# Cutting a key block's column products and summing product in two pieces each in a fused attention and Mish kernel

## The chip, the cores and the metric

The kernel runs on one core of a Trainium2 chip. The metric is the device time of one execution in microseconds (us), taken as the median of several runs.

## The reference

The input x is [1, 2048, 512]. One block normalises it and feeds two branches, which are multiplied and added back to x:

```python
xn = layernorm(x)                                   # over the 512 columns, no gain
q = (xn @ wq).reshape(1, 2048, 32, 16)              # 32 heads of 16
k, v = xn @ wk, xn @ wv                             # one key and one value head, 16 wide
p = softmax(einsum("bhqd,bkd->bhqk", q, k) * 16 ** -0.5)
s = (p @ v, heads side by side) @ wo
g = silu(mish(xn @ w1 + b1) @ w2)                   # 512 -> 1792 -> 512
out = x + s * g
```

All tensors are float32.

## The kernel before, in words

The work falls into a lead-in, 512 steps, and a short tail. A step (`s` in the code) takes one key tile of 128 keys for one unit; there are 32 units, each four heads by 512 queries. Per step TensorE computes four score products (tile `e`, line 1098), ScalarE turns them into exponentials (`pt`, line 1100), and TensorE multiplies the `pt` of two steps before with the values (`pv`, line 1187). The softmax needs row maxima ahead of the scores: TensorE computes score products a second time with the sides changed over (tile `m`, line 1119; the name `m_a_n` carries the half a and the count n) and VectorE takes the maximum of each (`mb`, line 1123), four per step, 20 steps ahead of their use.

Between these products TensorE works off groups of products for the other matrices (tile `xps`): query projections (weights `wq`), the first Mish matrix (weights `ws`, held in `early` for a while), the second (`wbs` with `act`), and the output matrix. A group has 12 or 15 products. In the lead-in each is one instruction over 128 rows (line 116). In the steps each is cut into two products over 64 rows (line 120), here called half-products, which share the array with an `m` or an `e` of the other 64 rows.

The lead-in loads x in four column blocks of 512 tokens (block 0 to 3), normalises (ScalarE, `xin`), transposes on TensorE (`xp`, line 302), copies the transposes into `xf` (line 320), and makes the keys and values of the block. For block 0 that is `k_proj`: four products into one bank. For blocks 1 to 3 it is

- `k_part` (line 336): 8 products with 32 output rows each, four column tiles of the array at a time, in two halves of 256 tokens, into the bank `kq`;
- `k_stage` (line 341): ScalarE copies `kq` to `vt`;
- `k_sum` (line 345): one product `ksum` x `vt` over 512 tokens into the bank `kp`, which adds up the four column tiles;
- `k_high` on ScalarE (line 356) and `k_low` on VectorE (line 239), which write the key block into `ks`; `v_copy`, `v_transpose` (`vp`) and `v_out` (`vaug`) for the values.

`kq`, `kp` and `vp` share one bank (`ps_v`). Maxima have three banks of their own (`ps_m`) and are taken in the order of the list `MSEQ`: eight of unit 0 on block 0, two of unit 1, then the rest of unit 0, eight to a key block, then unit 1. Each entry is a pair, one `m` for each half a. The lead-in ends when all 32 pairs of unit 0 are taken: VectorE makes the rows of maxima (`mp`, `cr`), eight DMAs carry them into `qt` (line 1174), and the first `e` can run.

What TensorE, ScalarE, VectorE, GpSimd and the DMA queue do in the lead-in, and in which order, is set by a planner at the end of the function. It holds tasks with an engine, an estimated duration and dependencies (`task(engine, us, function, deps, ...)`), keeps a clock `T` for each engine, and emits at each turn the task that can start first. A pair of maxima ("M") goes ahead of a task of TensorE when it may start no later; where TensorE has nothing for over 0.35 us by these estimates, the planner emits three products of the next group ("X") or, where no group is ready, a product whose result nobody reads (`warm`, line 1434). `bank(tag, n, t, users)` makes a task wait until the bank's earlier users are through. After the lead-in the order of the steps comes from other rules (`waves`), which take over the group where it stands.

```python
        if m is not None and (b is None or m <= b[0] + 0.05 or T["DVE"] < T["PE"] + 0.3 and m <= T["PE"] + 0.1):
            opts.append((m, "PE", "M"))
        elif b:
            opts.append((b[0], "PE", b[1]))
        e0 = min((o for o in opts if o[1] == "PE"), default=None, key=lambda o: o[0])
        low = min((o[0] for o in opts), default=None)
        if e0 is None or e0[0] > T["PE"] + 0.35:
            opts.append((T["PE"], "PE", "X"))
```

Of the kernel before, what the change touches and what calls it, by code (L numbers as in the profile page):

```python
# [14 lines left out]
F32 = mybir.dt.float32  # L15
# [5 lines left out]
P = 128  # L21
# [6 lines left out]
C = 512  # L28
# [98 lines left out]
def block_kernel(ctx: ExitStack, tc: tile.TileContext, x, wq, wk, wv, wo, w1, b1, w2, out):  # L127
# [5 lines left out]
    ps_v = ctx.enter_context(tc.tile_pool(name="ps_v", bufs=1, space=bass.MemoryType.PSUM))  # L133
# [4 lines left out]
    pe, act, dve, pool, sp = nc.tensor, nc.scalar, nc.vector, nc.gpsimd, nc.sync  # L138
# [27 lines left out]
    def sub(eng, o, a, b):  # L166
        ew(eng, o, a, b, ALU.subtract)
# [8 lines left out]
    def f(ap):  # L176
        return ap.bitcast(F32)
# [77 lines left out]
    def norm_a(z):  # L255
        if z.start >= 8:
            charge(0.25)
            pool.tensor_scalar(ve[:, z], mvs[:, z, 1], 1.0 / D if z.start >= A_LO else 1.0, EPS, op0=ALU.mult, op1=ALU.add)
        elif z.start >= A_LO:
            dve.tensor_scalar(ve[:, z], mvs[:, z, 1], 1.0 / D, EPS, op0=ALU.mult, op1=ALU.add)  # L260
        else:
            dve.tensor_scalar(ve[:, z], mvs[:, z, 1], EPS, None, op0=ALU.add)

    def norm_b(z):
        act.activation(rstd[:, z], ve[:, z], AF.Ln)
        act.activation(rstd[:, z], rstd[:, z], AF.Exp, scale=-0.5)

    def norm_c(z):
        r, h, b = rstd[:, z], hv[:, z], nbias[:, z]
        if z.start >= 8:  # L270
            charge(1.1)
            pool.tensor_tensor(out=h, in0=ve[:, z], in1=r, op=ALU.mult)
            pool.tensor_tensor(out=h, in0=h, in1=r, op=ALU.mult)
            pool.tensor_scalar(h, h, -0.5, 1.5, op0=ALU.mult, op1=ALU.add)
            pool.tensor_tensor(out=r, in0=h, in1=r, op=ALU.mult)
            if z.start < A_LO:
                pool.tensor_scalar(b, mvs[:, z, 0], -1.0, 0.0, op0=ALU.mult, op1=ALU.add)
            pool.tensor_tensor(out=b, in0=b, in1=r, op=ALU.mult)
            return
        stt(h, ve[:, z], -0.5, r, ALU.mult, ALU.mult)  # L280
        mul(dve, h, h, r)
        stt(r, h, 1.5, r, ALU.add, ALU.mult)
        if z.start >= A_LO:
            mul(dve, nbias[:, z], nbias[:, z], r)
        else:
            stt(nbias[:, z], mvs[:, z, 0], -1.0, r, ALU.mult, ALU.mult)

    def x_scale(t):
        x_ = xin[divmod(t, 4)]
        if t < 4 and t % 2:  # L290
            dve.tensor_scalar(x_, x_, rstd[:, t:t + 1], nbias[:, t:t + 1], op0=ALU.mult, op1=ALU.add)
        else:
            xn_scale(x_, x_, t)
# [3 lines left out]
    def x_transpose(t):  # L297
        c, tt = divmod(t, 4)
        ps, tag = (ps_m, "m") if t == 3 else (ps_e, "e")
        xp_of[t] = ps.tile([P, NDT, P], F32, tag=tag, name=f"xp{t}")  # L300
        for dt in range(NDT):
            pe.transpose(xp_of[t][:, dt], xin[c, tt][:, P * dt:P * (dt + 1)], ident)  # L302
# [7 lines left out]
    def x_high(t):  # L310
        act.activation(x_part(t, 0), xp_of[t], AF.Copy)
# [3 lines left out]
    def x_copy(t):  # L315
        c, tt = divmod(t, 4)
        if tt == 0:
            xf_of[c] = [sb.tile([P, 2, C], F32, tag="act", name=f"xf{c}_{k}", bufs=NACT) for k in range(2)]
        for k in range(2):
            act.activation(xf_of[c][k][:, :, P * tt:P * (tt + 1)], xp_of[t][:, 2 * k:2 * k + 2], AF.Copy)  # L320

    def x_low(t):
        sub(dve, x_part(t, 1), xp_of[t], f(x_part(t, 0)))

    vt_of = {}

    kp_of = {}
    kq_of = {}
    vp_of = {}

    def k_part(c):
        kq = ps_v.tile([P, C], F32, tag="v", name=f"kq{c}")
        for h in range(2):
            z = slice(C // 2 * h, C // 2 * (h + 1))
            for dt in range(NDT):
                pe.matmul(kq[32 * dt:32 * dt + 32, z], wkf[:, dt, P - 32:P], xf_of[c][dt // 2][:, dt % 2, z], start=True, stop=True)
        kq_of[c] = kq

    def k_stage(c):
        vt_of[c] = sb.tile([P, C], F32, tag=f"y{(2, 3, 1, 2)[c]}", name=f"vt{c}", bufs=1)  # L340
        act.activation(vt_of[c], kq_of[c], AF.Copy)

    def k_sum(c):
        kp_of[c] = ps_v.tile([P, C], F32, tag="v", name=f"kp{c}")
        pe.matmul(kp_of[c], ksum, vt_of[c], start=True, stop=True)

    def k_proj(c, dts):
        if 0 in dts:
# [30 lines left out]
    ksum = wkv[:, P:2 * P]  # L379
# [636 lines left out]
    def xt_keep(c):  # L1016

        xt_kept[c] = dram.tile([P, NDT, C], F32, tag=f"xt{c}", name=f"xtk{c}")
        for k in range(2):
            sp.dma_start(xt_kept[c][:, 2 * k:2 * k + 2], xf_of[c][k])  # L1020
# [284 lines left out]
    def task(eng, us, fn, deps=(), **kw):  # L1305
        t = Task(eng, us, fn, deps, **kw)
        plan[eng].append(t)
        return t
# [45 lines left out]
    def bank(tag, n, t, users):  # L1354

        b = used[tag]
        t.deps += (b[-n] if len(b) >= n else []) + (b[-1][:1] if b else [])
        b.append([t, *users])
# [7 lines left out]
    for c0, c1 in ((0, 1), (1, 2), (2, 3), (3, 4)):  # L1366
        z = slice(4 * c0, 4 * c1)
        na = task("POOL" if c0 >= 2 else "DVE", 0.3, lambda z=z: norm_a(z), st[z], prio=c0 and 1)
        nb = task("ACT", 0.45, lambda z=z: norm_b(z), [na])
        nrm = task("POOL" if c0 >= 2 else "DVE", 1.6 if c0 >= 2 else 0.8, lambda z=z: norm_c(z), [nb], prio=2 * c0 and 1)  # L1370
        for c in range(c0, c1):
            xs, scs = [], []
            for t in range(4 * c, 4 * c + 4):
                sc = task(*(("ACT", 0.72), ("DVE", 0.4))[c == 0 and t % 2], lambda t=t: x_scale(t), [nrm])
                scs.append(sc)
                tr = task("PE", 0.6, lambda t=t: x_transpose(t), [sc])
                if c == 0:
                    hi = task("ACT", 0.55, lambda t=t: x_high(t), [tr])
                    lo = task("DVE", 0.65, lambda t=t: x_low(t), [hi])
                    xf = task("ACT", 0.62, lambda t=t: x_copy(t), [hi], prio=1)  # L1380
                    if t < 3:
                        bank("e", 3, tr, [lo, xf])
                    xs.append(lo)
                    xs.append(xf)
                else:
                    lo = task("ACT", 0.62, lambda t=t: x_copy(t), [tr])
                    bank("e", 3, tr, [lo])
                    xs.append(lo)

            if c == 0:  # L1390
                def wq_low():
                    if not todo["wq"][0]:
                        split("wq")
                    it = items["wq"][0]
                    sub(dve, it.tile[:, 1], it.raw, f(it.tile[:, 0]))
                xs.append(task("DVE", 0.69, wq_low, scs))

                def q_first():
                    xt_done[0] = step[0]
                    lead["late"] = 2.9  # L1400
                    fill(12)
                    del lead["late"]
            else:
                def keep_x(c=c):
                    xt_keep(c)
                    landed(KEEP_US)
                task("SP", 1.0, keep_x, xs)
            if c == 0:
                qp = task("PE", 2.8, q_first, xs[0:8:2] + xs[8:])
                xs += [qp]  # L1410
            if c == 0:
                k0 = kp = task("PE", 0.9, lambda c=c: k_proj(c, (0,)), xs)
                for dt in range(1, 4):
                    kp = task("PE", 0.9, lambda c=c, dt=dt: k_proj(c, (dt,)), [kp], lat=0.0)
            else:
                kq = task("PE", 1.0, lambda c=c: k_part(c), xs)
                kg = task("ACT", 0.6, lambda c=c: k_stage(c), [kq])
                bank("v", 1, kq, [kg])
                k0 = kp = task("PE", 1.0, lambda c=c: k_sum(c), [kg])
            kv_done = kp  # L1420
            kh = task("ACT", 0.59, lambda c=c: k_high(c), [kp])
            kl = task("DVE", 0.68, lambda c=c: k_low(c), [kh])

            vc = task("ACT", 0.59, lambda c=c: v_copy(c), [kp])
            bank("v", 1, k0, [kl, vc])
            vtr = task("PE", 0.5, lambda c=c: (c == 1 and keep_warm(2), v_transpose(c)), [vc])
            vo = task("DVE", 0.22, lambda c=c: v_out(c), [vtr])
            bank("v", 1, vtr, [vo])
# [29 lines left out]
    while True:  # L1458
# [58 lines left out]
        elif k == "J":  # L1517
            tag = next((g for g in ("wq", "ws", "wb") if (g == "wq" or s > 19.0) and arrived(g) and busy[0] + E0 < s + 0.5), None)
# [37 lines left out]
    for s in range(NS + 2000):  # L1556
        inm = s < NS - LEAD
        if inm or cur["chunk"]:
            assert s < NS
            due(s)  # L1560
            h = s % 2
# [75 lines left out]
```

## Time and profile before

| | |
|---|---|
| median of 3 runs | 1576.33 us (1576.19 to 1576.45) |
| the profiled execution | 1576.55 us |
| its span, first to last instruction | 1574.4 us |
| granted TensorE clock | 1.000 |
| busy: TensorE / VectorE / ScalarE / GpSimd | 99% / 85% / 83% / 40% |
| TensorE instructions | 11738 |
| lead-in, to the first `e` | 78.2 us |

Rows of the timeline give the start, the duration, the engine, the line, the operation with its tiles and shapes, and the count of merged instructions; in brackets stands the idle time of that engine just before, and who ended it. A product of 512 columns in full float32 shows as two records.

### The profile page before, as it was taken

To read this page: it belongs to the slowest core of one execution; us is meant where nothing else is said; L and a number is where in the kernel's file an instruction comes from. 1 tells how busy PE (TensorE), PEld (TensorE's weight loads), DVE (VectorE), ACT (ScalarE), POOL (GpSimd) and SP (SyncE) were. 2 spreads that over 40 slices of the span, in tenths; PEclk is the share of its full clock that TensorE was granted. 3 is DMA by queue.
4 is the path that set the end of the run, shared out by engine and by line. 5 is a ranking of instruction groups with operands and counts; after the bars stand their busy time and mean duration, and the time that the engine had idled before them with its cause. 6 is when DMAs were issued, how large, how long until landed. Compare 5 with 4: busy or idle time off the path is not lost.

```text
span 1574.4 us, 31742 instructions
## 1 busy us (share of the span) xinstructions
PE 1562.6 (99%) x11738; PEld 842.0 (53%) x11738; DVE 1341.1 (85%) x2329; ACT 1307.8 (83%) x2518; POOL 633.7 (40%) x683
## 2 busy tenths in 40 slices
PE   9999999999999999999999999999999999999998
PEld 5555555555555555555555555555555555555554
DVE  8998888889889888888998988888889998888832
ACT  7588788798998779878989887887898878789886
POOL 4774266284464105503515320471251515126412
PEclk9999999999999999999999999999999999999999
DMA  6243231232331314122032222211332213032020
GB/s 191 93 124 112 65 101 44 60 118 84 125 97 41 103 44 137 45 69 83 24 100 65 64 93 69 85 59 30 112 99 85 74 40 111 19 111 58 15 81 28
DMA packets 74666, 124.31 MB, mean 79 GB/s; under 512 B 21520, under 2 KB 35344, under 8 KB 74512
## 3 DMA queue, kind: packets, MB, share of 16 engines
q1 hardware_dynamic: 74512, 122.29, 25.2%
q8 instruction: 93, 1.52, 0.4%
q14 instruction: 61, 0.50, 0.1%
HBM read 74.78 MB, written 26.21 MB: 64 GB/s over the span
## 4 chain that ended last, share of the span: by engine, by line
PE 95%; DVE 4%; ACT 1%; DMA 0%; issue 0%; SPq 0%; ACTq 0%; DVEq 0%
PE xps L120 44%; PE pv L1187 32%; PE e L1098 9%; PE m L1119 7%; DVE mb L1123 3%; PE late L120 1%; PE xps L116 0%; ACT pt L1100 0%; DMA xin<-in_dram 0%; PE late L1098 0%; PE kp L351 0%; PE wop L120 0%; PE xp L302 0%; PE late L116 0%; PE wop L116 0%
## 5 line engine op out<-in xcount | busy, mean ns | idle before, releaser
L1123 DVE TENSOR_REDUCE mb<-m 128x1 f32<-128x512 f32 x2048 | 1274.2, 683 | 171.3 <-PE m L1119 152.3
L1100 ACT ACTIVATE pt<-e 128x512 f32<-128x512 f32 x2018 | 1061.6, 602 | 220.7 <-PE e L1098 212.3
L1119 PE MATMUL m<-ks,qt 48*128 48x512 f32 (+1 forms) x2048 | 829.9, 421 | 1.6 <-DVE ks L239 0.5
L1098 PE MATMUL e<-qt,ks 64*128 64x512 f32 x2018 | 740.4, 401 | 0.3
L1187 PE MATMUL pv<-pt,vaug 128*32 128x512 f32 x4096 | 543.0, 604 | 0.0
L1119 PEld LDWEIGHTS m<-ks,qt 48*128 48x128 f32 (+1 forms) x2048 | 372.9, 185 | 55.7 <-DVE mb L1123 18.5
L1098 PEld LDWEIGHTS e<-qt,ks 64*128 64x128 f32 x2018 | 373.3, 186 | 17.9 <-ACT pt L1100 7.5
L120 PE MATMUL xps<-wbs,act 64*128 64x512 f32 x1248 | 339.1, 408 | 0.2
L120 PEld LDWEIGHTS xps<-wbs,act 64*128 64x128 f32 x1248 | 217.7, 185 | 177.4 <-ACT pt L1100 105.8
L120 PE MATMUL xps<-xt,ws 64*128 64x512 f32 x1104 | 305.8, 410 | 0.1
L120 PEld LDWEIGHTS xps<-xt,ws 64*128 64x128 f32 x1104 | 190.6, 185 | 182.7 <-ACT pt L1100 116.5
L174 POOL TENSOR_SCALAR t<-t 128x512 f32<-128x512 f32 x56 | 34.4, 615 | 395.1 <-ACT t L838 394.9
L1187 PEld LDWEIGHTS pv<-pt,vaug 128*32 128x32 f32 x4096 | 81.9, 108 | 137.4 <-issue 129.1
L164 POOL TENSOR_TENSOR hb<-hb,t 128x512 f32<-128x512 f32 x56 | 72.1, 1287 | 65.6 <-ACT t L851 52.4
L120 PE MATMUL xps<-xt,wq 64*128 64x512 f32 x336 | 93.2, 410 | 0.0
L120 PEld LDWEIGHTS xps<-xt,wq 64*128 64x128 f32 x336 | 58.0, 185 | 55.2 <-ACT pt L1100 35.2
L120 PE MATMUL xps<-wbs,ot_all 64*128 64x512 f32 x288 | 79.5, 409 | 0.0
L120 PEld LDWEIGHTS xps<-wbs,ot_all 64*128 64x128 f32 x288 | 49.6, 185 | 46.7 <-ACT pt L1100 29.3
L164 POOL TENSOR_TENSOR hb<-hb,u 128x512 f32<-128x512 f32 x56 | 72.3, 1291 | 4.4
L164 POOL TENSOR_TENSOR u<-u,t 128x512 f32<-128x512 f32 x56 | 71.8, 1282 | 4.7
L164 POOL TENSOR_TENSOR act<-hb,act 128x512 fp32r<-128x512 f32 x55 | 70.8, 1288 | 4.6
L159 POOL TENSOR_SCALAR qh<-qf 128x512 fp32r<-128x512 f32 x15 | 9.3, 620 | 111.8 <-ACT qf L770 76.2
(158 smaller groups left out, 954.9 us busy)
## 6 DMA issues: line engine op xcount, KB each, us to landing
wbs<-w SPq DMA_DIRECT2D x36, 512.0 KB
ws<-w SPq DMA_DIRECT2D x35, 512.0 KB
qt<-qh SPq DMA_DIRECT2D x256, 32.0 KB
w<-wbs SPq DMA_DIRECT2D x14, 512.0 KB
wq<-wq SPq DMA_DIRECT2D x14, 512.0 KB
wbs<-wo SPq DMA_DIRECT2D x12, 512.0 KB
rawws<-in_dram SPq DMA_DIRECT2D x21, 256.0 KB
rawwb<-in_dram SPq DMA_DIRECT2D x20, 256.0 KB
```

The lines of the kernel that those rows point to most:

```text
L120: i = self.pe.matmul(ps, self.lhs()[o], self.rhs()[o], start=(self.k == 0 and self.halves == 0), stop=(self.k == self.tot - 1 and self.hal ...
L159: pool.tensor_scalar(o, i, 1.0, 0.0, op0=ALU.mult, op1=ALU.add)
L164: eng.tensor_tensor(out=o, in0=a, in1=b, op=op)
L174: pool.tensor_scalar(o, o, lim, 0.0, op0=ALU.min, op1=ALU.max)
L1098: pe.matmul(e, ks[o:o + 64, P * k:P * (k + 1)], q[o:o + 64, p], start=True, stop=True)
L1100: r = act.activation(pt, e, AF.Exp, scale=0.25)
L1119: pe.matmul(m, q[o, p, P * t:P * (t + 1)], ks[o, C * kb:C * (kb + 1)], start=True, stop=True)
L1123: r = dve.reduce_max(out=mb_of[v][:, kb, z:z + 1], in_=m, axis=AX.X)
L1187: pe.matmul(o[32 * j:32 * j + 32], vaug[:, k], pt, start=(k == 0), stop=(k == 15))
```

## The change

`k_part` and `k_sum` take an argument `h` and issue one half, 256 tokens, each time. The planner gets two tasks of 0.5 us for each in place of one of 1.0 us, so that it may place other work of TensorE between the halves. The first half waits for what the whole waited for; `k_stage` still waits for both halves of `kq`, and `k_high` and `v_copy` for both halves of `kp`. This applies to blocks 1, 2 and 3.

```diff
-    def k_part(c):
-        kq = ps_v.tile([P, C], F32, tag="v", name=f"kq{c}")
-        for h in range(2):
+    def k_part(c, h):
+        if not h:
+            kq_of[c] = ps_v.tile([P, C], F32, tag="v", name=f"kq{c}")
+        kq = kq_of[c]
+        for h in (h,):
             z = slice(C // 2 * h, C // 2 * (h + 1))
             for dt in range(NDT):
                 pe.matmul(kq[32 * dt:32 * dt + 32, z], wkf[:, dt, P - 32:P], xf_of[c][dt // 2][:, dt % 2, z], start=True, stop=True)
-        kq_of[c] = kq
...
-    def k_sum(c):
-        kp_of[c] = ps_v.tile([P, C], F32, tag="v", name=f"kp{c}")
-        pe.matmul(kp_of[c], ksum, vt_of[c], start=True, stop=True)
+    def k_sum(c, h):
+        if not h:
+            kp_of[c] = ps_v.tile([P, C], F32, tag="v", name=f"kp{c}")
+        z = slice(C // 2 * h, C // 2 * (h + 1))
+        pe.matmul(kp_of[c][:, z], ksum, vt_of[c][:, z], start=True, stop=True)
...
-                kq = task("PE", 1.0, lambda c=c: k_part(c), xs)
+                k0 = task("PE", 0.5, lambda c=c: k_part(c, 0), xs)
+                kq = task("PE", 0.5, lambda c=c: k_part(c, 1), [k0], lat=0.0)
                 kg = task("ACT", 0.6, lambda c=c: k_stage(c), [kq])
-                bank("v", 1, kq, [kg])
-                k0 = kp = task("PE", 1.0, lambda c=c: k_sum(c), [kg])
+                bank("v", 1, k0, [kg])
+                k0 = task("PE", 0.5, lambda c=c: k_sum(c, 0), [kg])
+                kp = task("PE", 0.5, lambda c=c: k_sum(c, 1), [k0], lat=0.0)
```

The planner's other choices follow from this, so the order on every engine differs from block 1 on, until step 24, from which TensorE's order is the same to the end. In the rows below, the number after the last underscore is the tile's own; lines of the changed file stand some places further down.

TensorE in key block 2, before: the columns in one go, then one pair of maxima, the summing product, the next pair.

```order
L1119 MATMUL m_1_8_596<-ks,qt_77 128x512
L1434 MATMUL warm<-qt_79 128x512 x2
L336 MATMUL kq_611<-xf_0_526,wkf 32x256 x2
L336 MATMUL kq_611<-xf_1_527,wkf 32x256 x2
L336 MATMUL kq_611<-xf_0_526,wkf 32x256 x2
L336 MATMUL kq_611<-xf_1_527,wkf 32x256 x2
L1119 MATMUL m_0_9_620<-ks,qt_77 128x512
L1119 MATMUL m_1_9_623<-ks,qt_77 128x512
L345 MATMUL kp_629<-vt_626,wkv 128x512
L1119 MATMUL m_0_10_631<-ks,qt_77 128x512
L1119 MATMUL m_1_10_634<-ks,qt_77 128x512
```

The same block now:

```order
L338 MATMUL kq_629<-xf_0_529,wkf 32x256 x2
L338 MATMUL kq_629<-xf_1_530,wkf 32x256 x2
L1122 MATMUL m_0_11_635<-ks,qt_77 128x512
L1122 MATMUL m_1_11_638<-ks,qt_77 128x512
L338 MATMUL kq_629<-xf_0_529,wkf 32x256 x2
L338 MATMUL kq_629<-xf_1_530,wkf 32x256 x2
L1122 MATMUL m_0_12_648<-ks,qt_77 128x512
L1122 MATMUL m_1_12_651<-ks,qt_77 128x512
L348 MATMUL kp_656<-vt_646,wkv 128x256
L1122 MATMUL m_0_13_662<-ks,qt_77 128x512
L1122 MATMUL m_1_13_665<-ks,qt_77 128x512
L348 MATMUL kp_656<-vt_646,wkv 128x256
```

A pair of maxima stands between the halves of each, and the whole comes two pairs later; the two `warm` ahead of it are gone. In block 1 the halves are apart in the same way; there, two pairs of unit 1 and the transposes of two tiles of x have come ahead, and three `warm` stand where two stood, behind the pair `m_0_8`, `m_1_8` in place of the first pair of unit 1. On VectorE the `k_low` of block 1 stood ahead of the four maxima of unit 1 and now stands behind them. On ScalarE the first pass over a weight (`early<-rawws`, line 461), which waits for that weight's load, stood behind the `k_high` of block 2 and now stands ahead of it; on the DMA queue the store of block 2's `xf` (`xtk`) stood between two loads of weights and now stands ahead of both.

TensorE at the end of key block 3, before:

```order
L1119 MATMUL m_1_23_823<-ks,qt_77 128x512
L345 MATMUL kp_827<-vt_818,wkv 128x512
L116 MATMUL xps<-xt_216,wq_463 128x512 x6
L1434 MATMUL warm<-qt_79 128x512 x3
L1119 MATMUL m_0_24_846<-ks,qt_77 128x512
```

And now:

```order
L1122 MATMUL m_1_23_804<-ks,qt_77 128x512
L348 MATMUL kp_807<-vt_793,wkv 128x256 x2
L116 MATMUL xps<-xt_216,ws_554 128x512 x3
L1439 MATMUL warm<-qt_79 128x512 x2
L116 MATMUL xps<-xt_216,wq_463 128x512 x3
L1439 MATMUL warm<-qt_79 128x512 x3
L1122 MATMUL m_0_24_841<-ks,qt_77 128x512
```

Nothing stands between the halves here, since the maxima from 24 on need block 3 itself. Between `kp` and `m_0_24` stood six products of one group under way; now stand the last three of one group (`ws_554`) and the first three of the next (`wq_463`), which use the same bank.

Up to the first `e`, 75 whole products of groups stood before, 69 now. The steps make up for them. TensorE in step 20, its first part, before:

```order
L1098 MATMUL e_0_1928<-qt_78,ks 128x512
L120 MATMUL xps<-wbs,act_2_1094 128x512
L1119 MATMUL m_1_17_1933<-ks,qt_79 128x512
L120 MATMUL xps<-wbs,act_2_1094 128x512
L1098 MATMUL e_1_1937<-qt_78,ks 128x512
L120 MATMUL xps<-wbs,act_3_1311 128x512
L1098 MATMUL e_2_1942<-qt_78,ks 128x512
L1119 MATMUL m_0_16_1946<-ks,qt_79 128x512
L1098 MATMUL e_3_1949<-qt_78,ks 128x512
```

And now:

```order
L1101 MATMUL e_0_1922<-qt_78,ks 128x512
L120 MATMUL xps<-wbs,act_0_763 128x512
L1122 MATMUL m_1_17_1927<-ks,qt_79 128x512
L120 MATMUL xps<-wbs,act_1_931 128x512
L1101 MATMUL e_1_1931<-qt_78,ks 128x512
L120 MATMUL xps<-wbs,act_1_931 128x512
L1122 MATMUL m_1_18_1936<-ks,qt_79 128x512
L120 MATMUL xps<-wbs,act_1_931 128x512
L1101 MATMUL e_2_1940<-qt_78,ks 128x512
L120 MATMUL xps<-wbs,act_2_1212 128x512
L1122 MATMUL m_1_19_1945<-ks,qt_79 128x512
```

The half-products stand closer. Counted from the last `e` of a step to that of the next: 5 in each of steps 20 to 23 before, 8, 8, 7 and 7 now; 5 in steps 12 and 13 before, 6 now; 5, 5, 4 and 4 in steps 0 to 3 before, 3, 3, 6 and 6 now; all other steps have the same count in both (6 in steps 4 to 11 and 24 to 27, 5 in 14 to 19, and in 28 to 35 twice 8, 8, 7 and 7).

## The prediction

> **What bounds the kernel now.** The page first.
>
> ```profile
> PE 1562.6 (99%) x11738; PEld 842.0 (53%) x11738; DVE 1341.1 (85%) x2329; ACT 1307.8 (83%) x2518; POOL 633.7 (40%) x683
> ...
> PE 95%; DVE 4%; ACT 1%; DMA 0%; issue 0%; SPq 0%; ACTq 0%; DVEq 0%
> ```
>
> TensorE carries 95% of the chain that ended last, VectorE (DVE) 4%. The average hides two regimes, which the table of busy time by stretch shows.
>
> ```profile
> 25.00:78.00 53.00, 51.08 (x254) 27.81 (x253) 49.52 (x87) 35.55 (x79) 30.99 (x40) 1.00 0.34 106
> 400.00:600.00 200.00, 199.81 (x1536) 106.64 (x1536) 175.35 (x297) 165.73 (x318) 69.64 (x71) 1.00 0.29 92
> ```
>
> After the stretch come TensorE, its weight loads, DVE, ScalarE (ACT) and GpSimd. In the steps (400 to 600 us) TensorE never rests and DVE is busy 88%. In the lead-in DVE is at 93%, and TensorE's busy time holds `warm` products, which are fill. So there DVE's maxima set the pace. DVE's timeline, and its waits for maxima between 20 and 78 us:
>
> ```profile
> 25.26 8.89 DVE L1123 TENSOR_REDUCE mb<-m 128x1 f32<-128x512 f32 x14 [0.71 <-PE m L1119]
> 34.42 1.29 DVE L1123 TENSOR_REDUCE mb<-m 128x1 f32<-128x512 f32 x2 [0.27 <-PE m L1119]
> ...
> 41.33 1.29 DVE L1123 TENSOR_REDUCE mb<-m 128x1 f32<-128x512 f32 x2 [1.24 <-PE m L1119]
> 43.21 1.29 DVE L1123 TENSOR_REDUCE mb<-m 128x1 f32<-128x512 f32 x2 [0.59 <-PE m L1119]
> ...
> 47.66 13.58 DVE L1123 TENSOR_REDUCE mb<-m 128x1 f32<-128x512 f32 x22
> 61.16 0.74 DVE L239 SCALAR_TENSOR_TENSOR ks<-ks,ksgn,kp 112x512 fp32r<-112x512 f32 x1
> 62.48 2.48 DVE L1123 TENSOR_REDUCE mb<-m 128x1 f32<-128x512 f32 x4 [0.59 <-PE m L1119]
> ...
> 72.31 0.27 DVE L1154 TENSOR_REDUCE mp<-mb 128x16 f32<-128x64 f32 x1
> ```
> ```profile
> DVE mb L1123 <- PE m L1119: 3.4, 5, 1.2
> ```
>
> From the first maximum at 25.26 to the rows of maxima at 72.31 lie 47.05 us. In them DVE waits four times, 0.27 + 1.24 + 0.59 + 0.59 = 2.69 us (with the 0.71 before the start that is the 3.4 of the list). The other 44.36 us are work, the same pieces in both orders. So the lead-in changes by what the idle time changes, and by nothing else, as long as the rows of maxima release the end:
>
> ```profile
> 78.16 0.40 PE L1098 MATMUL e<-qt,ks 64*128 64x512 f32 x1
> ```
>
> The first `e` follows the rows by 5.85 us, through the eight DMAs of the rows and an order that stays.
>
> **The change, part by part.** What TensorE did around the four waits:
>
> ```profile
> 29.71 0.50 PE L1119 MATMUL m<-ks,qt 64*128 64x512 f32 x2
> 30.14 1.07 PE L336 MATMUL kq<-xf,wkf 128*32 128x256 f32 x16
> ...
> 32.84 1.13 PE L345 MATMUL kp<-vt,wkv 128*128 128x512 f32 x2
> 33.89 0.50 PE L1119 MATMUL m<-ks,qt 64*128 64x512 f32 x2
> ...
> 37.45 0.66 PE L302 MATMUL xp<-ident,xin 128*128 128x128 f32 x4
> 38.04 0.67 PE L1119 MATMUL m<-ks,qt 64*128 64x512 f32 x2
> 38.82 1.05 PE L1434 MATMUL warm<-qt 128*128 128x512 f32 x2
> 39.80 1.07 PE L336 MATMUL kq<-xf,wkf 128*32 128x256 f32 x16
> 40.80 0.49 PE L1119 MATMUL m<-ks,qt 64*128 64x512 f32 x2
> ...
> 58.76 1.97 PE L116 MATMUL xps<-xt,wq 128*128 128x512 f32 x6
> 60.56 0.85 PE L1434 MATMUL warm<-qt 128*128 128x512 f32 x3
> 61.95 0.50 PE L1119 MATMUL m<-ks,qt 64*128 64x512 f32 x2 [0.53 <-DVE ks L239]
> ```
>
> Units, start to start: a pair of maxima 0.43 us (29.71 to 30.14), columns 1.00 (39.80 to 40.80), summing product 1.05 (32.84 to 33.89), four transposes 0.59 (37.45 to 38.04). DVE needs 13.58 / 22 = 0.617 a maximum, 1.23 a pair. Halves cost 0.50 and 0.53 by division.
>
> *Block 2.* The 1.24 is two `warm` that wait for a maxima bank (38.82) plus the undivided columns. The 0.59 after it is the undivided summing product: 1.05 + 0.43 is over 1.23. Now each half plus a pair is 0.53 + 0.43 = 0.96, under 1.23: DVE stays fed and both waits go, -1.83.
>
> *Block 1.* The 0.27 goes too. What is late next: twice a half is followed by transposes ahead of the next pair, 0.53 + 0.59 + 0.43 = 1.55 against 1.23. The banks in hand cover some; I take 0.4 for both, bounds 0 and 0.6. Then `k_low` of block 1 now follows the four maxima of unit 1 on DVE, and the pair `m_0_8` waits for it, with those of blocks 1 and 2 queued behind it on TensorE. The same wait stands at 62.48, behind the `ks` at 61.16: 0.59. I take 0.6, bounds 0 and 0.75 (it would be less where a pair could pass). Behind that pair stand three `warm` (0.85 as at 60.56), `vp` and the next pair.
>
> ```profile
> 62.38 0.43 PE L372 MATMUL vp<-ident,vt 32*128 32x32 f32 x4
> ```
>
> With that, 0.85 + 0.43 + 0.43 = 1.71 against 1.23, and a `warm` can wait for a bank as at 38.82 (1.05 for two). I take 0.6, bounds 0.4 and 0.8. Block 1 together: 1.6 in place of 0.27.
>
> *Block 3.* Its halves stay together, and the 0.59 stays. But between them and `m_0_24` a group now ends and another starts in the same bank, so TensorE waits for ACT to empty it. ACT has `ks` and `vt` to do first:
>
> ```profile
> 60.07 0.59 ACT L367 ACTIVATE vt<-kp 32x512 f32<-32x512 f32 x1
> ...
> 70.86 0.69 ACT L830 ACTIVATE hb<-xps,b1c 128x512 f32<-128x512 f32 x1 [4.50 <-PE xps L116]
> ```
>
> On the times of before: 60.07 + 0.59 + 0.69 = 61.35, three products (half of 60.56 - 58.76) 0.90, three `warm` about 0.66: `m_0_24` at 62.9 in place of 61.95, 0.95 later. Busy rows overlap by some tenths, so I take 0.9: a wait of 1.5, bounds 0.59 (ACT is in time) and 2.0.
>
> Idle sum now: 1.6 + 0 + 1.5 = 3.1 against 2.69: lead-in +0.4. Bounds: 0.59 + 0.4 = 1.0, which is -1.7; 0.6 + 0.75 + 0.8 + 2.0 = 4.15, which is +1.5.
>
> *The steps.* In the lead-in the six products fewer save nothing, since TensorE there fills time that DVE sets. In the steps TensorE is the bound. The first row of `pv` in the timeline closes step 2, and each later one a step more; these close steps 7, 11, 23, 27 and 35.
>
> ```profile
> 100.52 1.06 PE L1187 MATMUL pv<-pt,vaug 128*32 128x512 f32 x8
> ...
> 111.91 1.07 PE L1187 MATMUL pv<-pt,vaug 128*32 128x512 f32 x8
> ...
> 146.28 1.06 PE L1187 MATMUL pv<-pt,vaug 128*32 128x512 f32 x8
> ...
> 157.66 1.07 PE L1187 MATMUL pv<-pt,vaug 128*32 128x512 f32 x8
> ...
> 182.11 1.06 PE L1187 MATMUL pv<-pt,vaug 128*32 128x512 f32 x8
> ```
>
> Four steps of 6 half-products took 11.39 (8 to 11) and 11.38 (24 to 27). Twelve of 5 (12 to 23) took 34.37, 11.46 for four. Eight of 8, 8, 7, 7 and again 8, 8, 7, 7 (28 to 35) took 24.45, 12.23 for four. So going from 5 to 6 in steps 12 and 13 costs nothing, and from 5 to 8, 8, 7, 7 in steps 20 to 23 costs 12.23 - 11.46 = 0.77. I take 0.8. Steps 0 to 3 go from 5, 5, 4, 4 to 3, 3, 6, 6, inside the range that costs the same. Bounds: 0.7, and 1.6 if the first steps lose as much again.
>
> [...] Between a maximum and `kq` or `kp` the array changes its tiling, and the split makes up to two more such changes at each of four split places. The `kq` at 30.14 starts 0.07 before the `m` ahead of it ends (29.71 + 0.50): no gap. [...] The trace shows no such gap, so nothing is added.
>
> Sum: +0.4 + 0.8 = +1.2. The profiled execution took 1576.55, 2.15 more than its span and 0.22 over the median; 1577.75 for it, **1577.5** for the median 1576.33.
>
> **The rivals.** 0.2% is 3.15 us, about what a measurement of this kernel can tell from no change: faster is under 1573.2, slower over 1579.5.
>
> *A: the waits go and nothing takes their place* (ACT is in time at block 3, blocks 1 and 2 run through): lead-in -1.7, steps +0.8, 1575.4. For it: halves of 0.5 under pairs of 1.23. Against: `k_low` behind four maxima. Even with all 2.69 gone and the six products free, 1573.6: this change cannot reach faster by 0.2%.
>
> *B: ACT is held by a load ahead of block 2's keys.* ACT's first pass over a weight now stands ahead of `k_high` of block 2, and that weight's load behind the 1 MB store of `xf`. Such a pair before:
>
> ```profile
> 56.24 0.80 SPq L1020 DMA_DIRECT2D xtk<-xf x2
> 57.14 2.79 SPq L514 DMA_DIRECT2D rawws<-in_dram x2
> ```
> ```profile
> 46.39 0.62 ACT L461 ACTIVATE early<-rawws 128x512 fp32r<-128x512 f32 x1
> 50.77 2.21 ACT L211 ACTIVATE xin<-xin,nbias,rstd 128x512 f32<-128x512 f32 x3
> 61.98 0.63 ACT L461 ACTIVATE early<-rawws 128x512 fp32r<-128x512 f32 x1 [1.31 <-DMA rawws<-in_dram]
> ```
>
> The load at 57.14 was there at 61.98, 4.84 later. With the store near 38 and the load near 39 it lands near 44, before the 46.39 at which ACT took it up. Each us beyond that moves block 3's `xin` (50.77), and with it the last keys, by one us. Slower by 0.2% needs another 2.0 over my 1.2, so a landing after 48.4, nearly twice the time measured. Then 1579.6 or more.
>
> *C: the halves cost nothing and gain nothing*: the lead-in as it was, 1577.1. This lies within my forecast.
>
> **How the numbers follow.** Forecast with C, 1576.4 to 1578.6: 0.66. A: 0.18. Block 1 and 3 at their upper bounds, to 1579.4: 0.08. B: 0.05. Anything else: 0.03. The range 1575.2 to 1579.2 takes in A and most of the upper bounds. Faster 0.02 (part of the unknown), slower 0.08 (B and what goes beyond the bounds), the same 0.90.
>
> **What would show it.** Right: no wait over 0.3 in block 2's `kq` and `kp`; waits near 0.6 before and behind `m_0_8`; over 1.0 before `m_0_24`, with TensorE held by ACT's `hb`; rows of maxima between 72 and 73.5; steps 20 to 23 at about 12.2 in place of 11.46. Wrong: rows of maxima before 71.5 (A) or after 74 (B), or steps after 24 at another pace than before, which no step of this argument allows.

## The result

The changed kernel took 1578.28 us (median of 22 runs, 1576.46 to 1586.13) against 1576.45 (22 runs, 1575.60 to 1580.04) before: a ratio of 1.0017, 95% interval 1.0009 to 1.0025. That is no change by the bound of 0.2%, but it is on the slow side and 0.8 us above the 1577.5 forecast. The profiled execution took 1578.51, its span 1576.7 in place of 1574.4.

The time outside the span, before the first instruction and after the last, is 2.13 us in the mean of the runs of the kernel before and 1.77 to 1.84 in the changed kernel and in each kernel of the experiments that is made from it. So some 0.34 us of a comparison with the kernel before lie outside what the profile orders, in the changed kernel's favour (the fifth experiment, made from the kernel before, has 2.14); no run shows where they come from.

The page after the change, busy time:

```profile
PE 1562.7 (99%) x11750; PEld 842.5 (53%) x11750; DVE 1339.9 (85%) x2329; ACT 1307.7 (83%) x2518; POOL 634.3 (40%) x683
```

TensorE's busy time is the same to 0.1 us. What grew is idle time of the lead-in, as DVE's waits there (us, times, the longest) and the table of busy time by stretch show (the figure ahead of the DMA share is the granted clock):

```profile
DVE mb L1126 <- PE m L1122: 5.5, 7, 1.7
```
```profile
25.00:78.00 53.00, 49.37 (x243) 26.91 (x244) 47.57 (x83) 34.76 (x77) 27.85 (x36) 0.97 0.34 106
40.00:50.00 10.00, 9.90 (x45) 4.55 (x44) 8.17 (x15) 5.42 (x15) 5.62 (x10) 0.83 0.44 136
```

DVE's waits for maxima went from 3.4 us to 5.5, and between 40 and 50 us the clock granted to TensorE was 0.83, where it had been 1.00 all through the lead-in before. DVE's timeline of the changed kernel:

```profile
25.43 7.46 DVE L1126 TENSOR_REDUCE mb<-m 128x1 f32<-128x512 f32 x12 [0.71 <-PE m L1122]
33.27 3.68 DVE L1126 TENSOR_REDUCE mb<-m 128x1 f32<-128x512 f32 x6 [0.38 <-PE m L1122]
37.24 1.29 DVE L1126 TENSOR_REDUCE mb<-m 128x1 f32<-128x512 f32 x2 [0.29 <-PE m L1122]
...
39.77 1.29 DVE L1126 TENSOR_REDUCE mb<-m 128x1 f32<-128x512 f32 x2 [0.58 <-PE m L1122]
42.00 1.29 DVE L1126 TENSOR_REDUCE mb<-m 128x1 f32<-128x512 f32 x2 [0.95 <-PE m L1122]
...
44.31 6.17 DVE L1126 TENSOR_REDUCE mb<-m 128x1 f32<-128x512 f32 x10 [0.89 <-PE m L1122]
...
64.39 2.48 DVE L1126 TENSOR_REDUCE mb<-m 128x1 f32<-128x512 f32 x4 [1.67 <-PE m L1122]
...
74.21 0.26 DVE L1157 TENSOR_REDUCE mp<-mb 128x16 f32<-128x64 f32 x1
```

From the first maximum to the rows of maxima it is 74.21 - 25.43 = 48.78 us, 1.73 more than the 47.05 before. The waits in it sum to 0.38 + 0.29 + 0.58 + 0.95 + 0.89 + 1.67 = 4.76 against 2.69. What TensorE did around those of blocks 1 and 2:

```profile
39.24 0.50 PE L1122 MATMUL m<-ks,qt 64*128 64x512 f32 x2 [1.44 <-DVE ks L239]
39.67 1.29 PE L1439 MATMUL warm<-qt 128*128 128x512 f32 x3
...
41.90 1.65 PE L116 MATMUL xps<-xt,ws 128*128 128x512 f32 x3
...
44.20 0.89 PE L338 MATMUL kq<-xf,wkf 128*32 128x256 f32 x8
```

TensorE idles 1.44 us ahead of `m_0_8`, because the pair waits for `k_low`. 2.7 us later three `xps` take 1.65 us, where three took 0.96 before; a half of `kq` takes 0.89, and the next half, at 45.48, only 0.64. In windows of 1 us the granted clock of this execution reads 1.00 up to 41 us, then 0.68, 0.50, 0.50 and 0.61, and 1.00 again from 45 on: 0.32 + 0.50 + 0.50 + 0.39 = 1.71 us lost, which is about 3.4 us at the lowest reading, 0.50. Block 2's wait of 0.89 ends within this stretch.

The steps: after the change, the rows that close steps 2, 19 and 23; then those of before that close steps 2 and 19 (that of 23 stands in the prediction, 146.28).

```profile
88.30 1.07 PE L1190 MATMUL pv<-pt,vaug 128*32 128x512 f32 x8
...
136.78 1.07 PE L1190 MATMUL pv<-pt,vaug 128*32 128x512 f32 x8
...
148.89 1.06 PE L1190 MATMUL pv<-pt,vaug 128*32 128x512 f32 x8
```
```profile
86.26 1.06 PE L1187 MATMUL pv<-pt,vaug 128*32 128x512 f32 x8
...
134.88 1.07 PE L1187 MATMUL pv<-pt,vaug 128*32 128x512 f32 x8
```

Steps 20 to 23 took 12.11 us, before 146.28 - 134.88 = 11.40: +0.71. So the profiled execution is 1.90 late at the rows of maxima (0.17 of it already at the first maximum), and 0.71 more is lost in the steps.

The 22 runs fall into groups by their mean granted clock: at 1.000 five runs of 1576.5 to 1577.3, at 0.998 eight of 1577.3 to 1578.5, at 0.997 six of 1579.4 to 1580.1, at 0.992 three of 1585.6 to 1586.1. The profiled execution, with one such slow stretch (1.71 us of 1576.7), is one of the eight at 0.998. All of them count as undisturbed in the ratio above.

### The profile page after: what moved, and what is told of

The parts are those of the page before. It is cut to its first block, busy times and chain, and to the rows that moved or that the text cites. A ratio compares the mean times of both kernels' runs of the same rounds, so it can differ in the third digit from the quotient of the medians.

```text
span 1576.7 us, 31761 instructions
## 1 busy us (share of the span) xinstructions
PE 1562.7 (99%) x11750; PEld 842.5 (53%) x11750; DVE 1339.9 (85%) x2329; ACT 1307.7 (83%) x2518; POOL 634.3 (40%) x683
## 4 chain that ended last, share of the span: by engine, by line
PE 96%; DVE 2%; ACT 1%; DMA 0%; issue 0%; SPq 0%; ACTq 0%; DVEq 0%
PE xps L120 45%; PE pv L1190 32%; PE e L1101 9%; PE m L1122 7%; DVE mb L1126 2%; PE xps L116 1%; PE late L120 1%; PE xp L302 0%; DMA xin<-in_dram 0%; PE late L1101 0%; ACT pt L1103 0%; PE kp L348 0%; PE kq L338 0%; PE kp L354 0%; PE wop L120 0%; PE late L116 0%
```

## The experiments

Two theories stood against each other. *Clock*: an idle TensorE in the lead-in is followed by a stretch at a lower clock, and that makes what the prediction did not foresee. *Queue*: all new waits come from the order of instructions alone. Each kernel ran 11 or 12 times, with the kernel before on the same chip (medians 1576.26 to 1576.54). A run "at a low clock" is one with a mean of 0.997 or less below; the changed kernel had 9 of 22, the kernel before 3 of the 92 in these comparisons. This bound leaves out runs with a single slow stretch, like the profiled execution of the changed kernel; the table in the last section gives the runs at 0.998 beside it.

**1. TensorE kept busy in block 1.** In the branch that issues a pair of maxima (`keep_warm` now takes the pool):

```
+            if MSEQ[m_next[0]] == (0, 8):
+                keep_warm(6, ps_e)
```

> The order of the changed kernel stays; six warm products (in a bank of e) fill TensorE's idle 1.44 us ahead of m_0_8 in block 1. Clock theory (an idle TensorE in block 1 lets the granted clock drop to 0.97 over 25 to 78 us, and the slow products that follow make block 2's unforeseen wait of 0.89 us): the granted clock over 25 to 78 is 1.00, the three xps behind the next pair take 0.96 us again and not 1.65, the wait before kq's first half falls from 0.89 to under 0.3; the waits of 0.58 and of 0.95 (at least 0.6 of it) stay, as does block 3's 1.67. Median 0.8 to 1.1 us below the changed kernel's 1578.3, so 1577.2 to 1577.5, and fewer runs at a mean clock of 0.998 or less. Queue theory (all new waits come from the order of instructions alone): no wait changes, 1578.3.

Measured: 1577.26 (1576.37 to 1578.14), ratio 1.0003 (0.9994 to 1.0012), no run below a clock of 0.999. The window, TensorE and DVE:

```profile
40.00:50.00 10.00, 9.71 (x50) 4.69 (x51) 9.22 (x17) 6.56 (x15) 5.58 (x10) 1.00 0.50 150
```
```profile
37.24 1.63 PE L1439 MATMUL warm<-qt 128*128 128x512 f32 x6
...
41.37 0.96 PE L116 MATMUL xps<-xt,ws 128*128 128x512 f32 x3
```
```profile
25.11 7.47 DVE L1126 TENSOR_REDUCE mb<-m 128x1 f32<-128x512 f32 x12 [0.71 <-PE m L1122]
...
39.46 1.29 DVE L1126 TENSOR_REDUCE mb<-m 128x1 f32<-128x512 f32 x2 [0.59 <-PE m L1122]
41.47 1.29 DVE L1126 TENSOR_REDUCE mb<-m 128x1 f32<-128x512 f32 x2 [0.72 <-PE m L1122]
...
62.93 2.48 DVE L1126 TENSOR_REDUCE mb<-m 128x1 f32<-128x512 f32 x4 [1.66 <-PE m L1122]
...
72.76 0.26 DVE L1157 TENSOR_REDUCE mp<-mb 128x16 f32<-128x64 f32 x1
```

Six products that compute nothing take 1.0 us off the median. The clock stays at 1.00, the `xps` take 0.96, and block 2 has no wait left; the wait behind the next pair shrinks from 0.95 to 0.72, the others stay. The stretch is 72.76 - 25.11 = 47.65: 1.13 less than in the changed kernel, and 0.89 + 0.23 of waits account for it. For the wait in block 2 this settles for the clock; the other new waits stay and belong to the order.

**2. The three warm products behind `m_0_8` left out.**

```
     def keep_warm(n=1):
 
+        if m_next[0] == 11:
+            return
```

> The three warm products behind m_0_8 in block 1 are left out; all else stands in the order of the changed kernel. Queue theory (the wait of 0.95 us is the time of these products, 1.29 us, in the queue ahead of the next pair): the wait of 0.95 falls to 0.2 or less, and the end with it: 1577.4 to 1577.6. Clock theory: TensorE now idles in two places close together; the clock falls at least as far as in the changed kernel (0.97 or less over 25 to 78), block 2's wait grows by a part or all of what the missing products save, and the median is 1578.0 to 1579.

Measured: 1577.83 (1575.55 to 1579.01), between the two forecasts; both medians were missed.

```profile
40.00:50.00 10.00, 9.96 (x43) 4.38 (x42) 8.91 (x16) 6.20 (x16) 5.79 (x11) 0.83 0.48 146
```
```profile
43.02 1.29 DVE L1126 TENSOR_REDUCE mb<-m 128x1 f32<-128x512 f32 x2 [0.64 <-PE m L1122]
44.75 4.93 DVE L1126 TENSOR_REDUCE mb<-m 128x1 f32<-128x512 f32 x8 [0.44 <-PE m L1122]
```

The wait of 0.95 is gone, as the queue theory says. The clock is 0.83 again, as the clock theory says, and block 2 waits 0.64 + 0.44 = 1.08 in place of 0.89. Both mechanisms are there; of the 0.95 that went, 0.19 came back as slower products.

**3. `k_low` of block 1 one pair earlier.** The planner holds the tenth pair until that task is ordered:

```
         v, n = MSEQ[m_next[0]]
+        if m_next[0] == 9 and kls[1].end is None:
+            return None
```

> The planner holds the second pair of maxima of unit 1 until block 1's k_low is ordered, so k_low stands one pair earlier on DVE and nothing holds m_0_8. The lead-in after it is planned anew (one pair stands between block 3's kp and the group behind it); the lead-in's number of products and all steps stay as in the changed kernel. Clock theory: no idle time of a us on TensorE in block 1, granted clock 1.00, the waits of 0.58 and 0.89 go and the 0.95 shrinks to 0.6: 1.8 us less, rows of maxima near 72.4, median 1576.4 to 1576.8, with 0.7 of the steps left in it. Queue theory: the 0.58 and 0.3 of the 0.95 go, the 0.89 of block 2 stays: 0.9 less, 1577.4.

Measured: 1579.16 (1576.01 to 1585.59), ratio 1.0021 (1.0010 to 1.0033). Four runs lie at 1576.0 to 1576.2, as expected, and eight between 1578.4 and 1585.6, all at a low clock. The cure of block 1 had made a longer idle time in block 3 (the profiled execution is one of the four, at 0.999):

```profile
60.92 0.97 PE L1122 MATMUL m<-ks,qt 64*128 64x512 f32 x6 [1.89 <-DVE ks L239]
```

**4. Block 3 undivided.** The columns and the summing product of block 3 are one task each again.

> Halves in blocks 1 and 2 alone; in block 3 the columns and the summing product are one task each. On TensorE the one difference in the lead-in is that no group ends between block 3's summing product and m_0_24: three products of the next group give way to three warm ones (six warm in a row). The prediction's step (TensorE held by ACT's hb, which must empty the bank of the finished group): the wait of 1.67 us before m_0_24 falls to 0.6, what k_low alone costs as before the change; rows of maxima near 73.1 in place of 74.2; median 1577.1 to 1577.4, if the three products taken out of the lead-in cost nothing in steps 0 to 3. Rival (the wait is TensorE's own queue, not ACT): six warm and three products take as long, the wait stays over 1.2 and the median at 1578.3. Either way block 1's and 2's waits and the clock stay as in the changed kernel.

Measured: 1578.45 (1576.12 to 1584.59), no better, though the profiled execution (span 1574.3, clock 1.000) shows in block 3 what was forecast. TensorE, then DVE:

```profile
59.16 1.66 PE L1445 MATMUL warm<-qt 128*128 128x512 f32 x6
61.34 0.49 PE L1122 MATMUL m<-ks,qt 64*128 64x512 f32 x2 [0.53 <-DVE ks L239]
```
```profile
61.85 2.48 DVE L1126 TENSOR_REDUCE mb<-m 128x1 f32<-128x512 f32 x4 [0.65 <-PE m L1122]
```

Without a group's end in front of it, `m_0_24` waits only for `k_low`, and DVE's wait is 0.65 in place of 1.67: the step on ACT's `hb` holds. The idle time in block 1 is untouched: TensorE waits 1.44 at 38.84 here too. But in this execution the clock stayed at 1.00, and block 2 has no wait of 0.89, the pair behind the warm products 0.72 in place of 0.95, and the rows of maxima come at 71.68, not near the 73.1 forecast. So those waits follow the clock and not the idle time by itself. Over the runs the clock varies: 3 of 11 runs lie at 1576.1 to 1576.7, six at 1578.2 to 1578.9 and two at 1583.7 and 1584.6. The median of such a mixture says little on a term of 1 us.

**5. The kernel before, with an idle time made in block 3.** The line `keep_warm(3)` ahead of `m_0_24` is taken out of the kernel before.

> The kernel before, without the change and without its three warm products ahead of m_0_24; nothing else moves. They end at 61.41 and m_0_24 waits for k_low until 61.95 either way, so by the order of instructions alone the time stays at 1576.5. Clock theory (idle TensorE in the lead-in of about a us is followed, in part of the runs, by a stretch at a lower clock): TensorE now idles 1.2 us ahead of m_0_24 in place of 0.53; at least a third of the runs show a mean clock of 0.998 or less and lie at 1577.5 or above, the others stay at 1575.6 to 1577.1; median 1576.8 to 1578.5. Rival (the low clock belongs to the halves, or to the chip on that day): the runs spread as those of the kernel before, at most one in ten above 1577.5.

```profile
61.99 0.49 PE L1119 MATMUL m<-ks,qt 64*128 64x512 f32 x2 [1.23 <-DVE ks L239]
```

Measured: 1576.43 (1575.27 to 1581.90). Three of twelve runs fell to a clock of 0.994 or 0.995 and took 1580.0 to 1581.9; the other nine lie at 1575.3 to 1577.0. That is a quarter, not the third or more expected, against 3 of 92; the median does not move. It points the same way without the halves being there, but three runs don't settle it alone.

**6. The third kernel with its idle time filled**: `keep_warm(10)` in place of `keep_warm(3)` ahead of `m_0_24`, and nothing else.

> As the third experiment (k_low of block 1 one pair earlier), with ten warm products in place of three ahead of m_0_24, which fill TensorE's idle 1.89 us there. In the third experiment the runs at a clock of 0.999 or 1.0 took 1576.0 to 1576.2, and two thirds of the runs lay 2 to 9 us higher at 0.990 to 0.997. Clock theory: those runs vanish, all or nearly all lie at 0.999 or above, median 1576.0 to 1576.5, no slower than the kernel before although steps 20 to 23 keep their 0.7. Rival (the low clock of the third experiment comes from elsewhere than that idle time): the spread stays, median above 1578.

```profile
58.37 2.47 PE L1441 MATMUL warm<-qt 128*128 128x512 f32 x10
61.02 0.96 PE L1122 MATMUL m<-ks,qt 64*128 64x512 f32 x6 [0.18 <-DVE ks L239]
```

Measured: 1575.87 (1575.11 to 1577.56), ratio 0.9996 (0.9987 to 1.0004). None of twelve runs is at a low clock, eight of twelve were in the third; three read 0.998 and took 1577.1 to 1577.6. Seven more products that compute nothing take 3.3 us off the median; the two kernels ran on different chips, on which the kernel before differs by 0.3. With the first experiment this is the second pair of kernels that differ in warm products alone.

**7. The summing product alone in halves**; the columns are one task again.

```
-                k0 = task("PE", 0.5, lambda c=c: k_part(c, 0), xs)
-                kq = task("PE", 0.5, lambda c=c: k_part(c, 1), [k0], lat=0.0)
+                k0 = kq = task("PE", 1.0, lambda c=c: (k_part(c, 0), k_part(c, 1)), xs)
```

> The summing product alone is halved; the columns stay one task. The lead-in holds 80 half-products as before the change, and the steps 5, 5, 5, 5 at 20 to 23. Prediction's step term: steps 20 to 23 take 11.4 us, not 12.1, and the pace from step 4 to step 35 is that of the kernel before. Lead-in: k_low of block 1 stands behind 18 maxima and not 20, so no wait of 0.58 at m_0_8; block 2 waits for its undivided columns (0.3 to 0.7 in place of 1.24), its 0.59 goes; block 3 keeps 0.6. No idle TensorE of a us, so no low clock. Median 1575.2 to 1576.2. Rival (halving costs by itself, at each change between products of different shape): no better than 1576.5.

Measured: 1575.11 (1574.56 to 1575.65, twelve runs), ratio 0.9990 (0.9981 to 0.9998): 1.15 us or 0.1% under the kernel before, with the interval clear of 1 but inside the 0.2% that counts as no change, and with the narrowest spread of all. 0.34 of the 1.15 lies outside the span. DVE, then the close of steps 19 and 23:

```profile
35.63 1.29 DVE L1126 TENSOR_REDUCE mb<-m 128x1 f32<-128x512 f32 x2 [0.29 <-PE m L1122]
...
41.78 5.00 DVE L1126 TENSOR_REDUCE mb<-m 128x1 f32<-128x512 f32 x8 [0.41 <-PE m L1122]
...
61.12 2.48 DVE L1126 TENSOR_REDUCE mb<-m 128x1 f32<-128x512 f32 x4 [0.59 <-PE m L1122]
70.94 0.27 DVE L1157 TENSOR_REDUCE mp<-mb 128x16 f32<-128x64 f32 x1
```
```profile
133.49 1.06 PE L1190 MATMUL pv<-pt,vaug 128*32 128x512 f32 x8
...
144.90 1.06 PE L1190 MATMUL pv<-pt,vaug 128*32 128x512 f32 x8
```

Block 2's 1.24 is 0.41 and its 0.59 is gone; block 1 keeps 0.29 and block 3 0.59. The rows of maxima come 1.37 earlier than before, and steps 20 to 23 take 144.90 - 133.49 = 11.41, as before the change, so nothing of it is given back by then. Products of other shape between maxima cost nothing that shows here: the median is 1575.11, where the rival had 1576.5 or more. By the rows 75 whole products of groups stand ahead of the first `e`, as before. (The expectations count in another way: 80 here, 78 in the eighth kernel and 84 in the tenth, where the rows have 72 and 78.)

But not all of this is the halved product's. Block 2's columns are undivided, and still 0.83 of their wait went, since three `xps` and a pair of maxima now stand where two `warm` stood right ahead of them (38.82 in the prediction's rows):

```profile
38.66 0.97 PE L116 MATMUL xps<-xt,ws 128*128 128x512 f32 x3
...
40.24 1.07 PE L338 MATMUL kq<-xf,wkf 128*32 128x256 f32 x16 [0.18 <-DVE vaug L378]
```

By these rows the halved summing product accounts for the 0.59, and the planner's new order for the 0.83. The eighth kernel has the same products ahead of its halved columns and no wait there, so halving the columns is worth the other 0.41. No run takes the two `warm` out and leaves everything undivided.

**8. The columns alone in halves**; the summing product's halves stand in one task.

> The columns alone are halved; the summing product's two halves stand in one task. Six warm products and 78 half-products in the lead-in, steps 12 and 13 get none, and steps 20 to 23 get 8, 8, 7, 7 as in the changed kernel. Prediction's step term: 20 to 23 take 12.1 us in place of 11.4, +0.7, and nothing comes back at steps 12 and 13, where TensorE is not what they wait for by more than some tenths. Lead-in: k_low of block 1 behind 18 maxima, block 2's 1.24 goes and its 0.59 at the summing product stays, block 3 0.6: 0.9 less than before the change. Median 1576.0 to 1576.8 if no idle TensorE lowers the clock. Rival for steps 12 and 13 (each half-product costs, whatever the step): 1575.5.

Measured: 1575.50 (1574.56 to 1579.98), ratio 0.9995 (0.9986 to 1.0004), at the rival's figure. Two of twelve runs are at a low clock; the profiled one is one of them (clock 0.62 over 60 to 78 us), so the end of its lead-in can't be read. Up to `m_0_24`, ahead of the slow stretch, DVE waits 0.38 + 0.28 + 0.36 + 0.30 + 0.58 = 1.90, 0.8 less than before, where 0.9 was forecast. Steps 20 to 23 take 149.90 - 137.80 = 12.10, as forecast. The rows close steps 11 to 13:

```profile
115.22 1.06 PE L1190 MATMUL pv<-pt,vaug 128*32 128x512 f32 x8
117.92 1.07 PE L1190 MATMUL pv<-pt,vaug 128*32 128x512 f32 x8
120.62 1.07 PE L1190 MATMUL pv<-pt,vaug 128*32 128x512 f32 x8
```

Steps 12 and 13, without half-products, take 2.70 each in place of 2.85: they give back 0.3, not nothing and not what five half-products would take. Of the other 0.2 to 1.0 by which it is under its forecast, 0.34 is the time outside the span.

**9. Three warm products in place of six** in the first experiment.

> As the first experiment with three warm products in place of six ahead of m_0_8, so that TensorE idles about 0.7 us there and not 1.44 (none with six). What it tells: how long the idle time must be before the low clock follows. With none of it, no run of the first experiment was over 1578.2; with all of it, 14 of the changed kernel's 22 runs were over 1578.0 and nine over 1579. If the length matters, 0.7 us behaves like the 0.53 of the kernel before: at most two runs over 1578.5, median 1577.0 to 1577.6. If any gap at this place does it, the spread of the changed kernel comes back, median above 1578.

```profile
39.52 0.50 PE L1122 MATMUL m<-ks,qt 64*128 64x512 f32 x2 [0.75 <-DVE ks L239]
```

Measured: 1577.65 (1576.96 to 1578.62). Two runs are over 1578.5 and none is at 0.997 or less, as forecast; the median lies just over its range and 0.4 above that of six products. But six of eleven runs read 0.998, where the first experiment has none and the kernel before 10 of 92, and the profiled execution is one of the six: its clock is 0.75, 0.50, 0.50 and 0.54 in the four us from 83 on, once more 1.71 us. That stretch stands behind TensorE's waits of 0.78 at 75.67 (for ACT) and 0.69 at 82.09 (for DVE). So a slow stretch can follow gaps of 0.7 to 0.8 us as well, and that 0.75 us acts like the 0.53 of before is not shown. The first experiment has both of the later waits too (0.78 and 0.70), without a run at 0.998.

**10. Halves in block 2 alone**, without the two warm products ahead of its columns.

> Halves in block 2 alone, where the prediction had both waits go; blocks 1 and 3 undivided, and the two warm products ahead of block 2's columns left out. Before the change these four places cost 0.27, 1.24, 0.59 and 0.59. By the prediction's unit sums (half and pair 0.96 against DVE's 1.23) block 2's two waits fall to 0.3 or less together, 0.27 and 0.59 stay: idle sum near 1.2, rows of maxima 1.2 to 1.5 us earlier. The lead-in holds 84 half-products, one later step gets none, and there are two stretches of 8, 8, 7, 7 as before the change: the steps cost the same within 0.2. Median 1574.6 to 1575.3, level with halving the summing product alone. Rival (idle TensorE ahead of block 2's columns, or a part of ACT's statistics that now stands ahead of its copy of kq, eats the gain): 1575.8 or more.

Measured: 1577.28 (1576.68 to 1578.21), a miss. Block 2 does as forecast: DVE has no wait there, 1.83 gone. TensorE in block 3, DVE there, and TensorE in a later step:

```profile
60.47 0.43 PE L375 MATMUL vp<-ident,vt 32*128 32x32 f32 x4 [0.77 <-DVE ks L239]
60.83 0.96 PE L1447 MATMUL warm<-qt 128*128 128x512 f32 x3
```
```profile
50.56 8.46 DVE L1126 TENSOR_REDUCE mb<-m 128x1 f32<-128x512 f32 x14 [0.46 <-PE m L1122]
59.67 0.75 DVE L239 SCALAR_TENSOR_TENSOR ks<-ks,ksgn,kp 112x512 fp32r<-112x512 f32 x1 [0.65 <-ACT vt L370]
...
62.26 1.29 DVE L1126 TENSOR_REDUCE mb<-m 128x1 f32<-128x512 f32 x2 [1.84 <-PE m L1122]
```
```profile
238.82 0.49 PE L1122 MATMUL m<-ks,qt 48*128 48x512 f32 x1 [0.52 <-DVE mb L1126]
```

The planner put `vp` and three warm products behind block 3's `k_low` and ahead of `m_0_24`: 1.84 in place of 0.59, which eats 1.25 of the 1.83. DVE also waits 0.46 at 50.56, for a pair, and 0.65 at 59.67, for ACT, which makes block 3's keys; neither wait was there before. So the idle sum is 0.29 + 0.46 + 0.65 + 1.84 = 3.24, more than the 2.69 before, and the rows of maxima come 0.52 later after the first maximum (47.57 against 47.05). The steps miss too: from the close of step 2 to that of step 35 it takes 182.42 - 86.05 = 96.37 against 95.85, and at 238.82 a step without half-products lets TensorE wait 0.52 for DVE. The rival's figure came; neither of its reasons is the main one.

## Why the prediction was right, and where not

The verdict, no change, and the range held. The working, step by step:

- *DVE's maxima set the lead-in*: right. In every kernel here the stretch up to the rows of maxima is DVE's waits (those of `k_low` for ACT with them) and 43.8 to 44.4 us of work.
- *The other 44.36 us are the same pieces in both orders*: off by 0.35. It is 48.78 - 4.76 = 44.02 in the changed kernel and 47.65 - 3.64 = 44.01 in the first experiment. About half of it is that the row of 14 maxima before (8.89) holds small gaps: 0.635 each against 7.46 / 12 = 0.622. The rest stays open.
- *Block 1, 1.6*: it was 0.38 + 0.29 + 0.58 + 0.95 = 2.20. The wait at `m_0_8` was forecast at 0.6 and was 0.58. The two at the halves (0.67) came out over their bound of 0.6, the one behind the warm products (0.95) over its bound of 0.8; 0.23 of the latter is the clock.
- *Block 2, both waits go*: true of the order. The first experiment shows no wait there. A half and a pair take 1.01 and 1.12 us there (from the halves' starts, 43.03 to 44.04 and 45.39 to 46.51), more than the 0.96 of the prediction, but still under DVE's 1.23. But of the 1.24 only 0.41 is the halves' and 0.83 that of the two `warm` that went (the seventh and the eighth). In the changed kernel a wait of 0.89 took their place, and this is the step that failed: the sum priced what DVE loses while TensorE waits for `k_low`, and not what TensorE's own idle time of 1.44 us does to the products behind it. No term and no rival had the clock: that cost was put at nothing, without a reason.
- *Block 3, 1.5 through ACT's `hb`*: 1.67, and the fourth experiment takes away the group's end and finds 0.65. TensorE's row of the changed kernel names the releaser:

```profile
62.26 0.97 PE L116 MATMUL xps<-xt,wq 128*128 128x512 f32 x3 [0.96 <-ACT hb L833]
```

- *Lead-in +0.4*: +0.60 with the clock held (47.65 against 47.05), +1.73 in the profiled execution. The difference of 1.13 is the clock's. That +0.60 is near +0.4 is in part luck: the idle sum came out at 3.64 and not 3.1, and the work 0.35 shorter, two errors that offset each other.
- *Steps 20 to 23, +0.8*: +0.71, and 0.01 where the lead-in keeps its 75 whole products (the seventh). That half-products in steps 0 to 3, 12 and 13 are free held as well: from the close of step 2 to that of step 19 it took 136.78 - 88.30 = 48.48 us against 134.88 - 86.26 = 48.62, and from the rows of maxima to the close of step 2 it took 14.09 against 13.95.
- *Changes of tiling between maxima and halves*, for which nothing was added: no run shows a cost of them where DVE waits. With halves between maxima block 2 had no wait at all in the first and tenth experiment.
- *Rivals.* A did not come: new waits took the place of the old ones, as the prediction argued. C is near what the first experiment shows for the order alone, +0.7. B did not come either: ACT's `k_high` of block 2 waited for the summing product, not for a load.

```profile
48.65 0.69 ACT L359 ACTIVATE ks<-kp,kone 112x512 fp32r<-112x512 f32 x1 [1.02 <-PE kp L348]
```

- *The signs.* By its own list the prediction would be wrong with the rows of maxima after 74, as a sign of B. They came at 74.21, and there was a wait of 0.89 in block 2 where none over 0.3 was allowed. The cause was not B: in the first experiment, with the clock held, the rows come at 72.76, between the 72 and 73.5 forecast.

So the mechanism of the order was right in the main. With the clock held (first experiment) the median span grows by 1.1 us (1575.5 against 1574.4), where +1.2 was forecast; the device time grows by only 0.72 (1577.26 against 1576.54 on the same chip), since 0.34 outside the span went. The remaining 1.0 us, up to 1578.28, is the clock, which the prediction had not seen. The range held because it was wide enough for that, not because it had foreseen it.

## What to carry to other kernels

Here an idle time of TensorE (1.44 us) that cost another engine 0.6 us cost more, 1.0 us of the median, through the products that followed it: price it twice, and look at the granted clock stretch by stretch, not at its mean. Where an instruction waited a us or more on TensorE (1.44 in the changed kernel, 1.89 in the third), products that compute nothing ahead of it were cheap cover (1.0 us off the median in the first experiment, 3.3 in the sixth), but only ahead of the wait; behind it, in front of what the bound engine needs, the same products are the wait (0.72 in the first, with the clock at 1.00). Splitting a long product helped where it alone starved the bound engine (in block 2, waits of 0.59 and 0.41); any split re-plans the work around it, for better (0.83 in the seventh) or worse (the tenth), and each new place has to be priced.

## What the runs showed of the hardware

An idle time of 1.4 to 1.9 us on TensorE was followed by a slow stretch in many runs but not in all. The table counts the runs by their mean clock; the idle time is that ahead of the pair that waits for `k_low`.

| idle time | kernel | runs at 0.998 | at 0.997 or less |
|---|---|---|---|
| 0.53 us, block 3 | before | 10 of 92 | 3 of 92 |
| 1.44 us, block 1 | changed | 8 of 22 | 9 of 22 |
| 1.44 us, block 1 | second | 5 of 11 | 2 of 11 |
| 1.44 us, block 1 | fourth | 3 of 11 | 5 of 11 |
| 1.89 us, block 3 | third | 0 of 12 | 8 of 12 |
| 1.23 us, block 3 | fifth | 0 of 12 | 3 of 12 |
| 0.75 us, block 1 | ninth | 6 of 11 | 0 of 11 |
| filled in block 1 | first | 0 of 11 | 0 of 11 |
| 0.18 us, block 3 | sixth | 3 of 12 | 0 of 12 |

A mean of 0.998 can hold one slow stretch, but need not: in the last 5 us, where the work runs out, the profiled executions read 0.66 to 1.00 as well, and the seventh has 4 of 12 runs at 0.998 that are no slower than 1575.7.

Four profiled executions have a slow stretch ahead of that. In all four the clock falls to 0.50. TensorE loses 1.71 us each time in the changed, the second and the ninth kernel, so the stretch lasts about 3.4 us at 0.50. In the eighth it loses four times as much: 0.70 in the window of 63 to 64 us, 0.50 in all 13 us from 64 to 77, 0.97 in the next, together 6.83 us:

```profile
60.00:78.00 18.00, 17.31 (x49) 8.65 (x49) 14.93 (x28) 3.94 (x7) 7.37 (x8) 0.62 0.22 60
```

That one stands behind an idle time of only 0.54 ahead of `m_0_24`, and TensorE is busy in 17.31 of the 18 us, so a short gap does not exclude a slow stretch and a busy TensorE does not end it at once. In the changed kernel the idle time ahead of the stretch was 1.44 us, between products that kept TensorE busy for the rest of the time from 25 to 40 us (13.56 + 1.44 = 15.00) and for 9.90 of the 10 us after that. How long an idle time it takes, and whether it is the cause each time, these runs do not show.
